# Causal mask of three chunks by ScalarE copies and GpSimd selects in place of VectorE products

## The chip, the cores and the metric

The kernel runs on one core of one Trainium2 chip. The metric is the device time of one execution in microseconds (us). Work is spread over TensorE (PE in the profile; its weight loads are PEld), VectorE (DVE), ScalarE (ACT), GpSimd (POOL) and the DMA queue of SyncE (SP). Each engine works its own queue in order and waits for others through semaphores.

## What is computed

A gated linear attention over 4 batches, 8 heads, 768 tokens and a head size of 48, followed by a two-layer block with hardswish on the 3072 tokens:

```python
for t in range(S):
    state = alpha[:, :, t, :, None] * state + einsum('bhd,bhe->bhde', k[:, :, t], v[:, :, t])
    y[:, :, t] = einsum('bhd,bhde->bhe', q[:, :, t], state)
x = y.transpose(0, 2, 1, 3).reshape(B * S, H * D)     # (3072, 384)
h = x @ w_in                                          # (3072, 2048)
g = h * clip(h + 3.0, 0.0, 6.0) / 6.0
out = g @ w_out                                       # (3072, 384)
```

## The kernel before

The 3072 tokens are cut into 24 chunks of 128 (`C`). A chunk `j` is six to a batch, and a chunk has two halves of 64 tokens (`HB`), `b` = 0 and 1. The 8 heads go as 4 pairs, `p` the pair and `a` the head in it. The recurrence is done by chunks: running products of `alpha` (scans on VectorE) scale `k` and `q`; inside a half, scores are a matmul of scaled `k` and `q`; what comes from earlier tokens goes through the state. The causal mask keeps a score only where the key's token is not later than the query's, so each 64x64 block of scores is multiplied by an upper triangle of ones.

Two chunks make a group `g` for the two matmul layers. Groups 0 and 1 run them plainly: `f` (L493) and `fa`, `fb` (L504) are pieces of the first layer, `fr` (L509, ScalarE) and `fg` (L513, VectorE) the hardswish, `b` (L531) pieces of the second. From group 2 on the first layer, and from group 1 on the second, use a scheme with fewer matmuls (`M`, L617; `P`, L720) and more sums on VectorE (`xc`, `y`, `o`, `s`, `x`). The weights come in as 64-bit floats and are turned to 32 bits on the chip in 16 slices (`w` loads; `d1`, `d2`, `dx` on ScalarE; `d3` on VectorE; `d4`, L216, on GpSimd) in the first 95 us.

All instructions follow one order written out by hand: a long string of words such as `m.3`, run under a manual schedule. Each word calls one step, and each engine gets its instructions in that order. The words that matter here:

- `sc.j.x.y`: scores of chunk j (L360) into PSUM banks x (heads a = 0) and y (a = 1) of four banks `t0` to `t3`
- `m.j`: the mask, `masked(j)` (L370), from these banks into the SBUF tile `A` (two buffers, `As`)
- `qa.j.b` (L380): copies of scaled `q` into the other partitions of `A`, on ScalarE
- `sv.j.b` (L433): copies of the state into the tile of `v`, on ScalarE
- `ya.j.x`, `yb.j` (L470): the matmuls of `A` and `v` for halves 0 and 1, into bank x; `cy` (L479) takes the result out
- `ta`, `tk`, `tq` (L283): transposes of alpha, k, q of the first six chunks into one of the same four banks; `ca` (L312) takes alpha out
- `u`, `sm`, `st`: update of the state (L444 on TensorE, L454 on VectorE, L423 on GpSimd)

`A` takes four mask products a chunk: one for each half b and head a, 64 partitions by 256 columns. Around the three changed steps the order reads (pieces left out at the dots):

```
... sv.3.0 qa.3.0 sm.3.0 w.9 f.0.6.3 qa.2.1 lk.5 d4.7 sv.3.1 tq.4.0 fb.0 m.3 sm.3.1 fr.0.1.0 ta.5.1 p.4
fg.0.1 d3.8 w.4 fr.0.5.1 ca.5 fg.0.5 fr.0.0.0 d1.8 ya.2.2 yb.2 w.10 d4.8 cy.2 fg.0.0 lq.5 ya.3.3 yb.3 cy.3
d2.9 la.6 f.0.7.2 ...
... sc.5.1.0 sc.4.3.2 u.4.3.0 u.5.1 d4.12 fa.4.3 d3.11 d4.11 m.4 fr.1.4.1 fr.1.2.0 f.1.5.0 fb.4 w.15 lq.6
sm.4.0 fg.1.2 b.0.0.1 ...
... d4.15 qa.5.1 m.5 kb.6.3 b.0.2 d4.14 P.1.0.0 sm.5.0 ...
```

Chunks 0 to 2 come before these, chunks 6 to 23 after them; the last product of the mask starts at 464.3 us.

Of the kernel before, what the change touches and what calls it, by code (L numbers as in the profile page):

```python
# [13 lines left out]
ALU = mybir.AluOpType  # L14
# [3 lines left out]
def kernel(  # L18
# [32 lines left out]
    nc = tc.nc  # L51
    B, H, S, D = q.shape
# [4 lines left out]
    NP = H // 2  # L57
# [5 lines left out]
    HB = C // 2  # L63
# [12 lines left out]
    mask = consts.tile([C, C], mybir.dt.bfloat16, tag="mask")  # L76
    make_upper_triangular(nc, mask, 1.0, diag=True)

    half = consts.tile([C, 1], FP, tag="half")
# [140 lines left out]
    R_t, P_t, Q_t, K_t, kb_t, A_t, xT_t, ps_t = ({} for _ in range(8))  # L220
# [131 lines left out]
    def scores(j, *at):  # L352
        sc = ps_t["sc", j] = [banks[i][:, 0 : NP * HB].rearrange("s (p t) -> s p t", p=NP)
                              for i in at]
        for p in range(NP):
            for b in range(2):
                half = slice(HB * b, HB * b + HB)
                for a in range(2):
                    r = slice(64 * a, 64 * a + D)
                    nc.tensor.matmul(sc[a][half, p], K_t[j][r, p, half], Q_t[j][r, p, half],  # L360
                                     start=True, stop=True)

    def masked(j):
        A_t[j] = As[j % 2]
        sc = ps_t.pop(("sc", j))
        for b in range(2):
            half = slice(HB * b, HB * b + HB)
            to = A_t[j][half, b].rearrange("s (p a) t -> s a p t", a=2)
            for a in range(2):
                nc.vector.tensor_tensor(  # L370
                    out=to[:, a], in0=sc[a][half],
                    in1=mask[half, half].unsqueeze(1).to_broadcast([HB, NP, HB]), op=ALU.mult)

    def place_q(j, b):
        if (j % NC, b) == (0, 0):
# [264 lines left out]
    def hidden1(g, o):  # L640
# [16 lines left out]
    b = {(i, k): w2[:, i * HF : (i + 1) * HF, k * HD : (k + 1) * HD]  # L657
         for i in range(2) for k in range(2)}
# [83 lines left out]
    def store2(g, i):  # L742
# [11 lines left out]
        "tq": lambda j, *i: transposed("q", j, *i), "ca": place_alpha, "r": decay, "p": growth,  # L754
        "k": lambda j: scaled("k", j), "q": lambda j: scaled("q", j),
        "sc": scores, "m": masked, "qa": place_q, "kb": k_by_token, "ck": keep_k,
        "st": decayed_state, "sv": place_state, "kt": turn_k, "kw": write_k, "kr": read_k,
        "u": update, "sm": next_state, "ya": lambda j, i: attend(j, 0, i),
# [196 lines left out]
```

## Time and profile before

| What | Value |
|---|---|
| Median of 3 runs | 530.98 us (530.96 to 531.14) |
| Profiled execution | 530.91 us, of which the span is 529.1 us |
| Instructions | 15082 |
| Granted TensorE clock (mean) | 0.999 |
| PE, PEld busy | 520.6 us (98%), 494.8 us (94%) |
| DVE, ACT, POOL busy | 462.0 us (87%), 259.6 us (49%), 55.3 us (10%) |
| Mask products, all chunks (L370) | 96, together 36.1 us |
| Mean rate of DMA | 103 GB/s |

The span runs from the first to the last instruction of the profiled execution; the time of the execution is somewhat longer. Busy time is the time in which an engine has an instruction in hand. Matmuls are pipelined and their ends modelled, so a full PE row has to be read together with the time that equal groups of matmuls take. In a timeline each line gives the start, the length, the engine, the line of the kernel, the operation with its tiles, and how often; a bracket at the end says how long the engine was idle before it and what ended that.

### The profile page before, as it was taken

To read this page: it belongs to the slowest core of one execution; us is meant where nothing else is said; L and a number is where in the kernel's file an instruction comes from. 1 tells how busy PE (TensorE), PEld (TensorE's weight loads), DVE (VectorE), ACT (ScalarE), POOL (GpSimd) and SP (SyncE) were. 2 spreads that over 40 slices of the span, in tenths; PEclk is the share of its full clock that TensorE was granted. 3 is DMA by queue.
4 is the path that set the end of the run, shared out by engine and by line. 5 is a ranking of instruction groups with operands and counts; after the bars stand their busy time and mean duration, and the time that the engine had idled before them with its cause. 6 is when DMAs were issued, how large, how long until landed. Compare 5 with 4: busy or idle time off the path is not lost.

```text
span 529.1 us, 15082 instructions
## 1 busy us (share of the span) xinstructions
PE 520.6 (98%) x6290; PEld 494.8 (94%) x6290; DVE 462.0 (87%) x838; ACT 259.6 (49%) x513; POOL 55.3 (10%) x89
## 2 busy tenths in 40 slices
PE   8799999999999999999999999999999999999997
PEld 6598886789999999999999999999999999999997
DVE  6998999999999999999999999899988896395471
ACT  4968875112755453464365355454353552543330
POOL 5333543100000100101000000000000000000000
PEclk9999999999999999999999999999999999999999
DMA  9998794213245365445452546153330214000001
GB/s 180 253 240 261 181 269 117 54 32 93 58 118 118 92 135 135 104 95 150 82 145 63 110 118 160 41 124 79 108 84 25 61 22 100 17 26 7 9 9 37
DMA packets 124100, 54.40 MB, mean 103 GB/s; under 512 B 83328, under 2 KB 116864, under 8 KB 124032
## 3 DMA queue, kind: packets, MB, share of 16 engines
q1 hardware_dynamic: 124032, 53.44, 42.8%
q8 instruction: 49, 0.80, 0.7%
q14 instruction: 19, 0.16, 0.1%
HBM read 44.50 MB, written 8.91 MB: 101 GB/s over the span
## 4 chain that ended last, share of the span: by engine, by line
PE 90%; DVE 4%; SPq 2%; DMA 2%; ACT 1%; issue 1%; POOL 0%; DVEq 0%; POOLq 0%; ACTq 0%
PE m_ps L720 36%; PE m_ps L617 31%; PE m_ps L493 6%; PE m_ps L531 4%; PE t_ps L470 4%; PE t_ps L360 2%; PE m_ps L504 2%; PE m_ps L548 2%; PE t_ps L444 1%; PE t_ps L283 1%; DMA rings<-in_alpha_dram 1%; DVE g_sb L554 1%; SPq L253 1%; PE t_ps L388 1%; SPq L410 0%
## 5 line engine op out<-in xcount | busy, mean ns | idle before, releaser
L720 PE MATMUL m_ps<-w,g_sb 128*128 128x192 f32 x704 | 121.8, 327 | 0.0
L623 ACT COPY g_sb<-m_ps 128x512 f32<-128x512 f32 x110 | 63.5, 583 | 116.6 <-PE m_ps L617 91.6
L720 PEld LDWEIGHTS m_ps<-w,g_sb 128*128 128x128 f32 x704 | 113.8, 190 | 0.5
L720 PE MATMUL m_ps<-rings,g_sb 128*128 128x192 f32 x528 | 91.3, 326 | 0.0
L720 PEld LDWEIGHTS m_ps<-rings,g_sb 128*128 128x128 f32 x528 | 85.4, 190 | 0.3
L617 PE MATMUL m_ps<-xc,w 128*128 128x128 f32 x640 | 82.1, 276 | 0.3 <-ACT g_sb L623 0.3
L617 PEld LDWEIGHTS m_ps<-xc,w 128*128 128x128 f32 x640 | 77.7, 192 | 1.2 <-ACT g_sb L623 0.4
L509 ACT ACTIVATE r<-g_sb,half 128x512 f32<-128x512 f32 x80 | 56.8, 721 | 36.3 <-DVE g_sb L558 17.5
L513 DVE SCALAR_TENSOR_TENSOR g_sb<-r,g_sb 128x512 f32<-128x512 f32 x80 | 53.8, 684 | 9.1 <-ACT r L509 8.7
L617 PE MATMUL m_ps<-xT,raw 128*128 128x128 f32 x400 | 53.2, 278 | 0.0
L617 PEld LDWEIGHTS m_ps<-xT,raw 128*128 128x128 f32 x400 | 48.8, 192 | 0.7 <-ACT g_sb L623 0.2
L664 DVE TENSOR_TENSOR g_sb<-g_sb 128x512 f32<-128x512 f32 (+1 forms) x55 | 42.2, 796 | 4.8 <-PE m_ps L720 4.5
L617 PE MATMUL m_ps<-xT,w 128*128 128x128 f32 x320 | 41.8, 277 | 0.0
L617 PEld LDWEIGHTS m_ps<-xT,w 128*128 128x128 f32 x320 | 39.0, 192 | 0.4
L380 ACT COPY A<-q 48x256 f32<-48x256 f32 x88 | 35.4, 402 | 2.9 <-PE t_ps L470 0.8
L370 DVE TENSOR_TENSOR A<-t_ps,mask 64x256 f32<-64x256 f32 x96 | 36.1, 415 | 0.4
L493 PE MATMUL m_ps<-xT,w 128*128 128x256 f32 x144 | 32.5, 381 | 0.0
L617 PE MATMUL m_ps<-xc,raw 128*128 128x128 f32 x240 | 31.9, 276 | 0.0
L321 DVE TENSOR_TENSOR_SCAN R<-t,ones 128x516 f32<-128x516 f32 x24 | 29.5, 1228 | 2.7 <-ACT t L312 2.7
L423 POOL TENSOR_TENSOR st<-sm,R 128x192 f32<-128x192 f32 x20 | 14.7, 737 | 157.2 <-DVE sm L454 157.1
L554 DVE TENSOR_TENSOR g_sb<-g_sb 128x512 f32<-128x512 f32 x40 | 26.9, 679 | 4.1 <-ACT g_sb L623 4.1
L554 DVE TENSOR_TENSOR g_sb<-m_ps,g_sb 128x512 f32<-128x512 f32 x30 | 20.5, 683 | 11.4 <-PE m_ps L617 7.0
(107 smaller groups left out, 718.2 us busy)
## 6 DMA issues: line engine op xcount, KB each, us to landing
raw<-in_moe_w_out_dram SPq DMA_DIRECT2D x8, 768.0 KB, 5.6
raw<-in_moe_w_in_dram SPq DMA_DIRECT2D x6, 768.0 KB, 6.8
v<-in_v_dram SPq DMA_DIRECT2D x48, 96.0 KB, 3.2
out_dram<-oh SPq DMA_DIRECT2D x44, 96.0 KB, 1.7
far<-kq SPq DMA_DIRECT2D x64, 64.0 KB, 2.2
kb<-far SPq DMA_DIRECT2D x64, 64.0 KB, 2.0
aq<-in_alpha_dram SPq DMA_DIRECT2D x36, 96.0 KB, 2.5
kq<-in_k_dram SPq DMA_DIRECT2D x36, 96.0 KB, 2.7
```

The costliest lines, as they stand in the source:

```text
L321: nc.vector.tensor_tensor_scan(out=reverse(R, n - 1, n), data0=reverse(ax, n, n), data1=reverse(ones, n, n), initial=0.0, op0=ALU.mult, op ...
L370: nc.vector.tensor_tensor(out=to[:, a], in0=sc[a][half], in1=mask[half, half].unsqueeze(1).to_broadcast([HB, NP, HB]), op=ALU.mult)
L380: nc.scalar.copy(out=to[:, a], in_=Q_t[j][64 * a : 64 * a + D, :, half])
L470: nc.tensor.matmul(y_of(j, (i + 1) // 2, p)[:, HB * b : HB * b + HB], vb[:, p, e : e + 32], A_t[j][:, b, 2 * p + a], start=(b == 0 and i = ...
L493: nc.tensor.matmul(h[:, f], w1[:, kk, o : o + C], xT_t[g][:, kk], start=(kk == 0), stop=(kk == KT - 1))
L509: nc.scalar.activation(out=to, in_=h, func=AF.Relu, bias=half, scale=1.0 / 6.0)
L513: nc.vector.scalar_tensor_tensor(out=to, in0=r, scalar=1.0, in1=h, op0=ALU.min, op1=ALU.mult)
L554: eng.tensor_tensor(out=out, in0=in0, in1=in1, op=ALU.add if s1 > 0 else ALU.subtract)
L617: nc.tensor.matmul(acc[g][i][:, f * C : (f + 1) * C], spots[w][:, f * C : (f + 1) * C], x_of(g, x), start=(first and f == 0), stop=last, s ...
L623: nc.scalar.copy(out=slots[z], in_=acc[g][i])
L664: nc.vector.tensor_tensor(out=out, in0=in0, in1=in1, op=ALU.subtract)
L720: nc.tensor.matmul(to[g], a, rhs[:, f], start=(first and f == 0), stop=(last and f == HF - 1), skip_group_check=True)
```

## The change

For chunks 3, 4 and 5, `masked` no longer multiplies scores by the mask on VectorE. ScalarE copies the unmasked scores from PSUM into `A` (four copies a chunk, same pieces of 64x256), and GpSimd then overwrites the entries of later keys with zero, in place, by two selects a chunk (one for each half, 64 partitions by 512 columns). GpSimd works only in SBUF here; so a chunk's 4 VectorE instructions become 4 of ScalarE and 2 of GpSimd. The order of words is the same, and the other 21 chunks are masked as before.

```diff
+    BY_SELECT = {3, 4, 5}
+
     def masked(j):
         A_t[j] = As[j % 2]
         sc = ps_t.pop(("sc", j))
...
             for a in range(2):
-                nc.vector.tensor_tensor(
-                    out=to[:, a], in0=sc[a][half],
-                    in1=mask[half, half].unsqueeze(1).to_broadcast([HB, NP, HB]), op=ALU.mult)
+                if j in BY_SELECT:
+                    nc.scalar.copy(out=to[:, a], in_=sc[a][half])
+                else:
+                    nc.vector.tensor_tensor(
+                        out=to[:, a], in0=sc[a][half],
+                        in1=mask[half, half].unsqueeze(1).to_broadcast([HB, NP, HB]), op=ALU.mult)
+        if j in BY_SELECT:
+            for b in range(2):
+                half = slice(HB * b, HB * b + HB)
+                nc.gpsimd.affine_select(out=A_t[j][half, b], in_=A_t[j][half, b],
+                                        pattern=[[0, H], [1, HB]], compare_op=ALU.is_ge, fill=0.0,
+                                        base=0, channel_multiplier=-1)
```

Lines behind the change lie 11 further down in the changed file (L380 becomes L391, and so on).

## The prediction

> **What bounds the kernel now.** First the page: busy times, their course over the span, and the chain that ended last.
>
> ```profile
> PE 520.6 (98%) x6290; PEld 494.8 (94%) x6290; DVE 462.0 (87%) x838; ACT 259.6 (49%) x513; POOL 55.3 (10%) x89
> ...
> PE   8799999999999999999999999999999999999997
> PEld 6598886789999999999999999999999999999997
> DVE  6998999999999999999999999899988896395471
> ...
> PE 90%; DVE 4%; SPq 2%; DMA 2%; ACT 1%; issue 1%; POOL 0%; DVEq 0%; POOLq 0%; ACTq 0%
> ```
>
> TensorE carries the chain; VectorE is as full as TensorE in the first half. Since matmul ends are modelled, a full PE row does not prove that PE is at its pace; the steps do. In the chain in order of time, 48 matmuls of L493 take 10.36 us (216 ns each), as 12 of them take 2.59 us elsewhere (216), and the groups of 16 at L720 take 2.60 us each nearly everywhere. So PE runs at its own pace, and time that it loses after the first 30 us comes back only from its few later stalls. The list of waits names those:
>
> ```profile
> PE t_ps L470 <- DVE s L454: 0.4, 1, 0.4
> PE m_ps L617 <- ACT g_sb L623: 0.3, 1, 0.3
> ```
>
> Columns: total us, times, longest. They lie at 183.25 us (0.36) and 275.90 us (0.25); together 0.6 us is all that a freer VectorE could win back. Then the timeline around m.3, the first changed step (start, us, engine):
>
> ```profile
> 46.82 0.58 ACT L392 COPY kb<-t_ps 128x512 f32<-128x512 f32 x1 [1.84 <-PE t_ps L388]
> ...
> 47.85 1.52 DVE L370 TENSOR_TENSOR A<-t_ps,mask 64x256 f32<-64x256 f32 x4
> ...
> 49.10 1.66 ACT L380 COPY A<-q 48x256 f32<-48x256 f32 x4
> ...
> 49.30 1.50 PE L504 MATMUL m_ps<-xT,w 128*128 128x128 f32 x12
> ...
> 50.64 0.60 PE L283 MATMUL t_ps<-ident,rings 128*128 128x128 f32 x4
> 50.78 0.73 ACT L433 COPY v<-s 48x192 f32<-48x192 f32 x2
> ...
> 51.17 1.99 PE L470 MATMUL t_ps<-A,v 128*32 128x64 f32 x128
> 51.53 1.26 ACT L509 ACTIVATE r<-m_ps,half 128x512 f32<-128x512 f32 x2
> ...
> 52.26 0.69 DVE L513 SCALAR_TENSOR_TENSOR g_sb<-r,m_ps 128x512 f32<-128x512 f32 x1 [1.36 <-ACT r L509]
> ```
>
> The reader should see that VectorE finished m.3 at 49.37, that ScalarE worked without a gap from 46.82 through 51.5, and that PE began ta.5.1 (L283) at 50.64 with no wait.
>
> **Step m.3: the one that costs.** Scores of chunk 3 lie in banks 2 and 1 (sc.3.2.1). ta.5.1 writes its four transposes into bank 1, and ya.2.2 behind it writes bank 2. Before, both banks were read out at 49.37, 1.27 us ahead of need. In the changed program the first transpose of ta.5.1 carries one more wait, on ScalarE: the last of the four copies reads bank 1.
>
> The queue decides when that is. m.3 stands behind qa.3.0, qa.2.1 and sv.3.1 in the order, so the copies follow the second L433 copy, which ends at 51.51. One copy is 64x256 from PSUM; no such row exists. Neighbours by size, ScalarE copies from PSUM: 128x192 takes 318 ns (L737), 128x384 480 (L479), 128x512 583 (L623), so 256 comes to about 370. Three L623 copies in a row take 1.56 us, one each 0.49, 0.09 less than their length: copies from PSUM overlap. L380 (48x256, SBUF) takes 402 ns and steps by 0.42. So the step is 0.28 to 0.42; I take 0.28, since the source is PSUM: 51.45 + 3 x 0.28 + 0.37 = 52.66; with the upper value 51.53 + 3 x 0.42 + 0.40 = 53.19. PE restarts 0.05 to 0.2 us after such a releaser (VectorE's k at 18.87 let L388 go at 18.92; its s at 183.10 let L470 go at 183.25). That gives 52.7 to 53.4 in place of 50.64: a stall of 2.1 to 2.75 us. I take 2.25, near the PSUM rows.
>
> What else is late at that point, and is it later than PE?
> - The gate fr.0.1.0 (L509) waits behind the four copies: from 51.53 to about 52.75. Its product fg.0.1 (L513) releases bank m2 for f.0.7.2 (L493 at 53.09); before, product end (52.95) and matmul start were 0.14 apart. The release comes at 52.75 + 1.42 = 54.2. PE gets there at 52.9 + 0.44 (ta) + 1.92 (L470, as in the chain) = 55.25. Covered by 1 us; without that cover it alone costs 1.2 us, the lower bound of this step.
> - The two selects. The first starts after copy 2, at 52.1; ya.3 needs it, yb.3 needs the second. Nearest rows: the setup's affine select of 128x128 takes 292 ns, a memset of 128 columns 204, of 1024 columns 951. With the memset's fixed part of 97 ns, the select costs 1.52 ns a column, so 512 cost 0.88 us; a memset of 64x512 takes 0.52 (lower end), and two-input L216 of 768 columns takes 1.46 to 2.65, or 1.0 to 1.77 for 512 (upper end). I take 0.9, by the select's own row. The second then ends at 53.95, and PE reaches yb.3 at 52.9 + 0.44 + 0.96 + 0.48 = 54.8. Covered by 0.8 us; it comes through from 1.3 us a select on.
> - ScalarE and VectorE themselves are set back by about 1.2 us (VectorE's freed 1.5 us only lengthens its wait of 1.36 us on L509), less than PE. GpSimd's next L216 (d4.8, 55.14) starts after the selects.
>
> **Steps m.4 and m.5: nothing either way.** The copies of m.4 wait for sc.4 (L360 at 75.36 plus 1.16, now 2.25 later) and stand ahead of fr.1.4.1 and fr.1.2.0, and sm.4.0 on VectorE now waits for them; the product fg.1.2 slips by 2.25 plus 0.2 to 0.6 to about 82.3. Its bank m1 is wanted by b.0.0.1, at 82.5 + 2.25: 2.4 us in hand. ScalarE has 2.82 us idle at 82.73 and takes up the rest; A of chunk 4 is not read until 111.5. GpSimd's d4.13 (83.91), queued behind these selects, starts after they end; SP's queue is unchanged. The copies of m.5 fall into ScalarE's idle 9.03 us before 98.67, the selects into GpSimd's 3.35 us before 93.82. VectorE is freed of 1.52 us at 93.61 and then waits on PE at 119.99, as it already did for 1.37 us:
>
> ```profile
> 119.99 0.36 DVE L740 TENSOR_TENSOR oh<-m_ps,p 128x192 f32<-128x192 f32 x1 [1.37 <-PE m_ps L720]
> ```
>
> There VectorE is back where it was against PE, so the stalls at 183 and 276 us stay. PE has no stall between 53 and 119 us that the freed 3 x 1.52 = 4.6 us of VectorE could take away; they are worth 0.
>
> **Sum.** The profiled execution took 530.91 us, of which 529.1 is the span and 1.8 lies around it; the median of the runs is 530.98, 0.07 more. 530.9 + 2.25 = 533.2 us.
>
> **Rivals.**
> - *Selects on the path.* At 1.77 us each the second ends at 52.1 + 3.54 = 55.65, yb.3 starts 0.85 late, total stall 3.1: 534.1; with the upper copy step 534.6. Against it: the setup's two selects start 0.24 us apart. For it: the same L216 takes anything from 1.46 to 2.65 us. Chance 0.12.
> - *Clock.* PE's first 4.8 us ran at half pace: four transposes took 0.85 us in the chain at 4.81, later 0.44. If a pause brings that back for as long, it costs some 2.4 us more: 535.6. Against it: between 17.9 and 21.26 us PE stood still for 1.02 and then 1.46 us, and the four transposes after that took 0.63 in the timeline against 0.60 in flow. Chance 0.04.
>   The Trainium skill, "TensorE: Matmul & The Clock Gate", Part 1, puts the return to half clock at an idle window of about 3.4 us; by that rule this gap is too short, and the trace agrees as far as its own pauses go.
> - *Faster.* VectorE is 98% busy from 60 to 100 us (19.71 and 19.68 of 20 us). Were it the true bound there, with PE's row full only by modelled ends, the 3.0 us freed by m.4 and m.5 would count and m.3 would cost only ScalarE's 1.2: 529.1. It decides if PE waits unseen for VectorE between 60 and 119 us; against it stand the equal steps of 216 ns and no such wait in the list. Chance 0.05.
>   The Trainium skill, "Perfetto Trace Analysis", Optimizing Scalar/DVE Operations, holds that a saturated VectorE may be relieved onto ScalarE or even GpSimd; here that helps only if this rival is right.
> - *No loss.* The stall is made good later, if PE's later order has slack that I do not see, or ScalarE reaches the copies earlier: 530.9 to 531.9. Against it: ScalarE had no gap from 46.82 on, PE next to none after 53. Chance 0.09.
>
> **How the numbers follow.** My forecast has 0.70, with its own range of 532.4 (the stalls at 183 and 276 vanish) to 533.7 (slow copies). Selects take the top to 534.8. Out of 531.8 to 534.8 fall the clock, the faster case and most of "no loss", with edges under 0.2. A change under 0.2% (1.06 us) cannot be told from none: faster 0.05, same 0.09, slower 0.86.
>
> **What would show it.** Right: a wait of PE at L283 on ScalarE's new copies, 2.1 to 2.75 us long and ending near 53, the only new one in the list; L493 at 55.3 in place of 53.09, and everything of PE after that shifted by the same amount; ScalarE copies stepping by about 0.28. Wrong: L470 waiting on GpSimd there (selects), L493 groups of 12 above 2.59 us after the gap (clock), fewer than 2 us lost by PE at 119, or PE ahead of its old times after 95 (VectorE was the bound).

## The result, and the profile after

The changed kernel takes 533.09 us (median of 5 runs, 532.74 to 533.89) against 530.98 us (530.58 to 531.45): 2.11 us more, a ratio of 1.0042 with a 95% interval of 1.0027 to 1.0057. The profiled execution took 533.60 us, its span is 531.9.

The page after, the lines that answer to those of before:

```profile
PE 521.8 (98%) x6290; PEld 495.5 (93%) x6290; DVE 460.8 (87%) x826; ACT 263.4 (50%) x525; POOL 60.6 (11%) x95
...
PE 87%; DVE 4%; DMA 3%; SPq 2%; ACT 2%; issue 1%; DVEq 0%; POOL 0%; ACTq 0%; POOLq 0%
```

PE has the same 6290 matmuls and almost the same busy time (521.8 against 520.6 us). VectorE lost 12 instructions, and its mask products fell from 36.1 to 31.6 us, yet its busy time fell by only 1.2 us; the last section says where most of the rest went. The waits of PE after (total us, times, longest):

```profile
PE t_ps L283 <- ACT A L373: 1.9, 1, 1.9
...
PE t_ps L481 <- DVE s L465: 0.4, 1, 0.4
PE m_ps L628 <- ACT g_sb L634: 0.2, 1, 0.2
```

The first line is new, and is the transposes of ta.5.1 waiting for chunk 3's copies. The other two are the stalls near 183 and 276 us, still there. The timeline of the changed kernel around m.3 (11 lines have been added, so L380 is L391, L470 is L481, L493 is L504):

```profile
49.67 1.65 ACT L391 COPY A<-q 48x256 f32<-48x256 f32 x4
...
49.87 1.50 PE L515 MATMUL m_ps<-xT,w 128*128 128x128 f32 x12
...
51.33 0.71 ACT L444 COPY v<-s 48x192 f32<-48x192 f32 x2
51.95 1.29 ACT L373 COPY A<-t_ps 64x256 f32<-64x256 f32 x4
52.65 1.38 POOL L381 TENSOR_SCALAR_AFFINE_SELECT A<-A 64x512 f32<-64x512 f32 x2 [2.80 <-ACT A L373]
53.27 1.27 ACT L520 ACTIVATE r<-m_ps,half 128x512 f32<-128x512 f32 x2
...
53.30 0.66 PE L283 MATMUL t_ps<-ident,rings 128*128 128x128 f32 x4 [1.92 <-ACT A L373]
...
53.88 1.99 PE L481 MATMUL t_ps<-A,v 128*32 128x64 f32 x128
53.99 0.69 DVE L524 SCALAR_TENSOR_TENSOR g_sb<-r,m_ps 128x512 f32<-128x512 f32 x1 [3.04 <-ACT r L520]
...
55.81 2.43 PE L504 MATMUL m_ps<-xT,w 128*128 128x256 f32 x10
```

The copies follow the last L444 copy at once and end at 53.24; PE starts 0.06 us later. The 12 matmuls of L515 ahead of this start at 49.87, which is 0.57 us later than before: that much of this one execution was lost earlier. So ta.5.1 is late by 53.30 - 50.64 - 0.57 = 2.09 us on account of the change. The list gives its wait as only 1.92 us, because a wait is counted from the end of the matmuls before it (51.37), and undisturbed ta.5.1 began 0.16 us ahead of that end (50.64 against 49.30 + 1.50). At the other end the loss is unchanged: VectorE's L740, which stood at 119.99, is at 122.67 here, 2.68 later, of which 2.11 after taking off the 0.57.

### The profile page after: what moved, and what is told of

Its sections match the earlier page's. It is cut to its first block, busy times and chain, and to the rows that moved or that the text cites. A ratio compares the mean times of both kernels' runs of the same rounds, so it can differ in the third digit from the quotient of the medians.

```text
span 531.9 us, 15095 instructions
## 1 busy us (share of the span) xinstructions
PE 521.8 (98%) x6290; PEld 495.5 (93%) x6290; DVE 460.8 (87%) x826; ACT 263.4 (50%) x525; POOL 60.6 (11%) x95
## 4 chain that ended last, share of the span: by engine, by line
PE 87%; DVE 4%; DMA 3%; SPq 2%; ACT 2%; issue 1%; DVEq 0%; POOL 0%; ACTq 0%; POOLq 0%
PE m_ps L731 36%; PE m_ps L628 31%; PE m_ps L504 5%; PE m_ps L542 4%; PE t_ps L481 4%; PE t_ps L360 2%; PE m_ps L515 2%; SPq L253 1%; PE t_ps L455 1%; DMA rings<-in_q_dram 1%; DMA rings<-in_alpha_dram 1%; DVE g_sb L565 1%; PE t_ps L283 1%; ACT A L391 1%; PE t_ps L399 1%
## 5 line engine op out<-in xcount | busy, mean ns | idle before, releaser
L628 PE MATMUL m_ps<-xT,raw 128*128 128x128 f32 x400 | 53.2, 278 | 0.0
L675 DVE TENSOR_TENSOR g_sb<-g_sb 128x512 f32<-128x512 f32 (+1 forms) x55 | 43.5, 819 | 4.8 <-PE m_ps L731 4.5
L391 ACT COPY A<-q 48x256 f32<-48x256 f32 x88 | 35.4, 402 | 2.6 <-PE t_ps L481 0.8
L504 PE MATMUL m_ps<-xT,w 128*128 128x256 f32 x144 | 32.5, 381 | 0.0
L375 DVE TENSOR_TENSOR A<-t_ps,mask 64x256 f32<-64x256 f32 x84 | 31.6, 414 | 0.3
```

What stands on the lines that cost most here:

```text
L375: nc.vector.tensor_tensor(out=to[:, a], in0=sc[a][half], in1=mask[half, half].unsqueeze(1).to_broadcast([HB, NP, HB]), op=ALU.mult)
L391: nc.scalar.copy(out=to[:, a], in_=Q_t[j][64 * a : 64 * a + D, :, half])
L504: nc.tensor.matmul(h[:, f], w1[:, kk, o : o + C], xT_t[g][:, kk], start=(kk == 0), stop=(kk == KT - 1))
L628: nc.tensor.matmul(acc[g][i][:, f * C : (f + 1) * C], spots[w][:, f * C : (f + 1) * C], x_of(g, x), start=(first and f == 0), stop=last, s ...
L675: nc.vector.tensor_tensor(out=out, in0=in0, in1=in1, op=ALU.subtract)
```

## The experiments

Two theories were to be told apart. *Queue*: the loss is PE's one wait at ta.5.1, because the copies stand late in ScalarE's order. *Selects*: GpSimd's part costs, by late tiles or by slowing VectorE beside it. All ratios are to the kernel before on the same chip.

**Which chunk.**

```diff
-    BY_SELECT = {3, 4, 5}
+    BY_SELECT = {4, 5}      # e1_only_4_5
+    BY_SELECT = {3}         # e2_only_3
```

> Chunk 3 is masked on VectorE again; 4 and 5 by copies and selects. Queue theory (the loss is PE's one wait of 1.9 to 2.1 us for chunk 3's copies, which stand late in ScalarE's order): no wait at the transposes of ta.5.1, time of before, 530.8 to 531.3. Rival theory (GpSimd's selects cost, by slowing VectorE's instructions beside them or by late tiles, in all three chunks alike): two thirds of the loss stay, 532.3 to 532.6. Rival that VectorE was the true bound at 60 to 100 us: faster, 528 to 530.

> Only chunk 3 by copies and selects. Queue theory: the whole loss is there, 532.9 to 533.4, with the same wait of PE at ta.5.1. Select theory: one third of the loss, 531.5 to 531.9.

Measured: e1_only_4_5 531.02 us, ratio 0.9998 (0.9986 to 1.0010); e2_only_3 533.32 us, ratio 1.0046 (1.0033 to 1.0060). Chunk 3 alone has the whole loss; chunks 4 and 5 cost and bring nothing that shows (the interval of e1_only_4_5 runs from 0.7 us less to 0.5 us more). PE waits 1.9 us for the copies in e2_only_3, and not at all in e1_only_4_5.

**The same copies elsewhere in ScalarE's order.** `mc.3` is the four copies, `ms.3` the two selects, which stay where `m.3` was.

```diff
-    ... d4.6 ck.4 sm.2.1 st.3 d2.8 ...            tq.4.0 fb.0 m.3 sm.3.1 ...
+    ... d4.6 ck.4 sm.2.1 st.3 mc.3 d2.8 ...       tq.4.0 fb.0 ms.3 sm.3.1 ...   # e3_copies_before_d2
+    ... d4.6 sm.2.1 mc.3 ck.4 st.3 d2.8 ...       tq.4.0 fb.0 ms.3 sm.3.1 ...   # e4_copies_before_ck
```

> All three chunks as in the changed kernel, but chunk 3's four copies stand earlier in ScalarE's order: ahead of d2.8, where ScalarE has no idle time after them; the selects stay where they were. Queue theory: banks 1 and 2 are read out at about 48.7, so ta.5.1 doesn't wait; but everything of ScalarE behind them comes 1.25 us later, the gate fr.0.1.0 too, and so f.0.7.2 waits for its bank m2: PE loses 1.2 in place of 2.1 us, 532.0 to 532.4. If the loss were the selects': as the changed kernel, 533.1. If a late gate costs nothing: 531.0.

> As the changed kernel, but chunk 3's four copies stand ahead of ck.4 (and sm.2.1 ahead of them), where ScalarE was idle for 1.84 us before the change; the selects stay where they were. Queue theory: four copies take 1.3 us, so nothing behind them is late and no bank is: time of before, 530.8 to 531.4, with all 12 VectorE products still gone. Select theory: as the changed kernel, 533.1. If VectorE were the bound anywhere behind: faster than before, under 530.

Measured: e3_copies_before_d2 532.24 us, ratio 1.0018 (1.0005 to 1.0030); e4_copies_before_ck 530.89 us (530.59 to 533.29), ratio 0.9999 (0.9985 to 1.0013). The loss of e3_copies_before_d2 is 1.0 us by the ratio (0.3 to 1.6) and 1.3 us by the medians. Its timeline (two lines further down again, so L493 is L506):

```profile
47.08 1.30 ACT L373 COPY A<-t_ps 64x256 f32<-64x256 f32 x4
...
50.41 0.60 PE L283 MATMUL t_ps<-ident,rings 128*128 128x128 f32 x4
...
52.51 1.26 ACT L522 ACTIVATE r<-m_ps,half 128x512 f32<-128x512 f32 x2
53.23 0.69 DVE L526 SCALAR_TENSOR_TENSOR g_sb<-r,m_ps 128x512 f32<-128x512 f32 x1 [3.04 <-ACT r L522]
...
53.97 0.70 PE L506 MATMUL m_ps<-xT,w 128*128 128x256 f32 x2 [0.86 <-DVE g_sb L526]
```

ta.5.1 no longer waits; now the late gate holds bank m2, and PE waits there. In e4_copies_before_ck the copies run in what was ScalarE's idle time ahead of `ck.4` (L392 before, L405 here), and nothing behind is late:

```profile
44.84 1.29 ACT L373 COPY A<-t_ps 64x256 f32<-64x256 f32 x4
...
46.43 0.58 ACT L405 COPY kb<-t_ps 128x512 f32<-128x512 f32 x1 [0.31 <-PE t_ps L401]
```

The same 12 copies and 6 selects then cost nothing. Nor do the 12 products taken from VectorE bring anything.

**The selects.** Left out altogether, and three times for chunk 3.

```diff
-        if j in BY_SELECT:                                   # before the selects
+        if False:                                            # e5_no_selects
...
+                for _ in range(3 if j == 3 else 1):          # e6_selects_3x
                     nc.gpsimd.affine_select(...)
```

> The changed kernel without any select: chunks 3 to 5 keep scores of later keys. Queue theory: time unchanged, 532.9 to 533.4, same wait at ta.5.1. Select theory: back to 531.0. In the trace, VectorE's two-input sums that ran beside selects (the L692 pair at 93.6, 1.74 us in the changed kernel) should take their 1.29 us again.

> Each select of chunk 3 is issued three times (the repeats change nothing). In the changed kernel the two selects end at 54.03 and yb.3 needs the second at 55.32, so 1.3 us of cover. Six selects at 0.70 us a step from 52.65 end at 56.85: yb.3 waits 1.5 us, 534.4 to 534.9, with PE waiting on GpSimd at L481. If selects overlap or are never waited for: 533.1.

Measured: e5_no_selects 533.23 us, ratio 1.0043 (1.0031 to 1.0055): the selects as they are cost nothing. e6_selects_3x 537.41 us, ratio 1.0126 (1.0109 to 1.0142): they do cost once they are long enough. PE then waits for them at yb.3:

```profile
57.57 0.65 PE L482 MATMUL t_ps<-A,v 128*32 128x64 f32 x32 [1.27 <-POOL A L382]
```

But the time is some 2.5 us above what was expected.

**The copies twice**, which lengthens the wait of ta.5.1; the gate and the selects move with it.

```diff
+                    for _ in range(2 if j == 3 else 1):
                         nc.scalar.copy(out=to[:, a], in_=sc[a][half])
```

> Each copy of chunk 3 is issued twice. Queue theory: the last one ends 4 steps of 0.31 us later, so PE waits 3.1 to 3.3 us at ta.5.1 in place of 1.9 to 2.1: 534.2 to 534.6. If something else released ta.5.1: 533.1.

Measured: 536.03 us (534.88 to 537.38), ratio 1.0097 (1.0082 to 1.0112). The wait grew to 3.5 us, a little more than expected: the eight copies took 2.89 us, 0.36 a step, where each piece is written twice in a row. That accounts for 0.2 to 0.4 of the excess over 534.2 to 534.6 us. In the profiled execution (537.21 us) the rest is in the clock. Two-microsecond stretches of e7_copies_2x (busy time of PE, PEld, DVE, ACT, POOL, then granted clock, DMA share, GB/s):

```profile
52.00:54.00 2.00, 0.00 (x0) 0.00 (x0) 0.00 (x0) 1.88 (x7) 0.66 (x1) 0.80 1.02 387
54.00:56.00 2.00, 1.81 (x36) 1.48 (x39) 1.12 (x2) 1.98 (x5) 0.66 (x1) 0.50 1.21 216
56.00:58.00 2.00, 2.00 (x84) 2.00 (x80) 1.93 (x4) 1.73 (x3) 0.14 (x1) 0.50 1.18 160
58.00:60.00 2.00, 2.00 (x38) 1.65 (x28) 0.82 (x2) 1.05 (x2) 1.62 (x3) 0.50 0.08 20
```

The granted clock fell to a half at 53.2 us, still in the pause, and was back at full at 60.0. The profiled executions of e5_no_selects and e6_selects_3x show one such spell after their pause of 1.9 us, here e5_no_selects:

```profile
54.00:56.00 2.00, 2.00 (x88) 2.00 (x82) 1.93 (x4) 2.00 (x4) 0.00 (x0) 0.50 1.17 258
56.00:58.00 2.00, 2.00 (x48) 1.75 (x41) 1.72 (x3) 1.36 (x4) 1.35 (x1) 0.67 1.31 167
```

and its 128 matmuls of L481 took 3.47 in place of 1.99 us. That execution took 534.95 us and another 534.75; the other four of the six were at 532.67 to 533.38. In e2_only_3, 8 of 12 executions lie at 532.77 to 533.53 and 4 at 534.16 to 534.77; the five of the changed kernel all lie at 532.74 to 533.89. So 6 of 23 executions with the pause of 1.9 us are in an upper group. Only one of the six was profiled, so that the other five had the same spell is inferred. Without this pause such stragglers are rarer: 2 of all 74 executions of the kernel before (532.35 and 534.56), 1 of 12 of e4_copies_before_ck (533.29).

**VectorE freed for nothing.** Chunks 4 and 5 without any mask, all else as before; this leaves out part of the computation.

```diff
-    BY_SELECT = {3, 4, 5}
+    BY_SELECT = set()
...
-            for a in range(2):
+            for a in range(0 if j in (4, 5) else 2):
```

> The kernel before, but chunks 4 and 5 have no mask products at all (their part of A keeps old values), which frees VectorE of 3.0 us around 77 and 94 us and gives no engine anything in exchange. Queue theory (TensorE is the bound there): within 0.3 us of before, 530.7 to 531.3. Rival that VectorE is the bound between 60 and 100 us: up to 3 us faster, 528 to 529.

Measured: 530.91 us, ratio 0.9998 (0.9989 to 1.0006). The mask products fell by 3.0 us where VectorE is 98% busy. About half of that came back, because two sums now ran beside GpSimd (last section): VectorE's busy time fell from 462.0 to 460.4 us. Still 1.6 us were freed, and the time does not move; the interval leaves at most 0.6 us.

**The pause filled.** Matmuls on the identity into bank t3, whose result nobody reads, ahead of ta.5.1 (n = 4, 7, 4 and 2).

```diff
+    def fill(n):
+        for _ in range(n):
+            nc.tensor.matmul(banks[3].rearrange("p (a c) -> p a c", c=C), ident,
+                             ident.unsqueeze(1).to_broadcast([C, 4, C]), start=True, stop=True)
...
-    ... fr.0.1.0 ta.5.1 ...
+    ... fr.0.1.0 zt.n ta.5.1 ...
```

> The changed kernel, with four matmuls of 128x512 on the identity into the unused bank t3 ahead of ta.5.1: they keep TensorE busy for 1.7 us of its wait for the copies, and their result is never read. Clock theory (some executions lose a further 1.7 us because the pause halves the clock for about 3.4 us; executions of e2_only_3 and e5_no_selects fall into two groups, 532.7 to 533.5 and 534.2 to 534.95): time at the lower group, 532.7 to 533.4, and no granted clock under 1.00 between 50 and 62 us. If the upper group has another cause (DMA, VectorE): two groups again.

> Chunk 3's copies twice, as in e7_copies_2x, with seven such filling matmuls (3.0 us) ahead of ta.5.1. Clock theory: the wait of 3.5 us stays and the half clock after it goes: 534.3 to 534.7, against 536.0 without filling. Otherwise: 536.0 as before.

> Chunk 3's selects three times, as in e6_selects_3x (537.4), with four filling matmuls ahead of ta.5.1. Clock theory: without half clock the two waits of 1.9 and 1.3 us and the restarts after them remain, and since PE then gets to yb.3 earlier its wait for GpSimd grows to 2.3 us at most: 534.3 to 535.6, no execution above 536. Otherwise: 537.4.

Measured: e9_fill 534.54 us (534.29 to 535.37), ratio 1.0068 (1.0055 to 1.0082); e10_copies_2x_fill 536.96 us (536.82 to 537.10), ratio 1.0111 (1.0098 to 1.0125); e11_selects_3x_fill 535.90 us (535.43 to 536.10), ratio 1.0090 (1.0076 to 1.0104). The filling was mis-sized: each product became two instructions of 0.43 us, so four took 3.4 us and seven 6.0, and both ran past the copies. The timeline of e9_fill:

```profile
51.15 3.60 PE L564 MATMUL t_ps<-ident 128*128 128x512 f32 x8
...
54.59 0.60 PE L283 MATMUL t_ps<-ident,rings 128*128 128x128 f32 x4
```

So e10_copies_2x_fill does not answer its question, but it gives the price of lateness alone: counted from the 12 matmuls ahead of it, ta.5.1 starts 6.0 us late (56.81), and the time is 6.0 us longer, at a mean granted clock of 1.0 (0.999 once). And e9_fill tells what was asked, against e7_copies_2x. Behind matmuls ta.5.1 starts 3.4 us late, and this costs 3.6 us (3.3 to 4.4) at a mean granted clock of 1.0 in each of the 5 executions. Behind a pause it starts 3.7 us late, and this costs 5.1 us (3.9 to 6.4) at 0.994 to 0.997. In e11_selects_3x_fill, too, the median falls by 1.5 us against e6_selects_3x, though PE there reaches yb.3 no earlier and waits 1.2 us for the same selects. It lies above the 534.3 to 535.6 that were expected, and two of its four executions are above 536.

> As e9_fill, but half the filling: a 128x512 product on the identity turned out to be two instructions of 0.43 us each, so two of them fill 1.7 us (four took 3.4 and ran past the copies). ta.5.1 then waits about 0.4 us more for the copies. Clock theory: 532.7 to 533.5 in every execution, none at 534.2 or above, granted clock 1.00 from 50 to 62 us. If the upper group has another cause, some executions are above 534 again.

Measured: 533.22 us (532.69 to 533.73), ratio 1.0041 (1.0027 to 1.0055); PE waits 0.2 us for the copies behind the filling. No execution of the five is above 534 (533.73, the longest, is a little above the 533.5 expected), and the granted clock is 1.00 from 50 to 62 us in the profiled one. Filled or not, the changed kernel's normal loss is the 2.1 us of late copies; what the filling seems to take away is the chance of a spell of half clock behind it. Five executions without one are weak evidence by themselves, where 6 of 23 are in the upper group.

## Why the prediction was right, point by point

- *Bound.* "PE runs at its own pace" held: e8_no_mask_4_5 and e1_only_4_5 are both at 0.9998, and their intervals leave at most 0.7 us of gain. The rival that VectorE was the true bound, with a time of 529.1 us, is refuted.
- *The place.* The new wait of ta.5.1 on the last copy of m.3, with the copies behind qa.2.1 and sv.3.1, is what the profile shows, and chunk 3 alone carries the loss.
- *The size.* With the 0.57 us of the start taken off, the copies run from 51.38 to 52.67 (forecast 51.45 to 52.66), step 0.31 (0.28), length 367 ns (370). PE restarts 2.09 us late; 2.25 had been taken, 0.16 too much. From an end at 52.66 the 2.25 us mean a restart after 0.23 us, outside the prediction's own 0.05 to 0.2; PE followed after 0.06. The sign that was named, a wait of 2.1 to 2.75 us in the list, came out as 1.92, for the reason told with the result. L493, forecast for 55.3, is at 55.81 - 0.57 = 55.24. That it fits so well is partly luck: the restart was set 0.16 us too late, and ta.5.1 was given 0.44 us where it took 0.58 (53.30 to 53.88).
- *Cover.* The gate was covered: its product ends at 54.68 - 0.57 = 54.11 (forecast 54.2), 1.1 us ahead of L493. Without that cover it costs by itself: 1.2 us forecast, 1.0 by the ratio and 1.3 by the medians in e3_copies_before_d2. The selects take 0.69 us each in place of 0.9 and were covered with more to spare.
- *m.4 and m.5.* Nothing, as forecast, but one term was wrong. VectorE was to be freed of 1.52 us at 93.61 and to spend it waiting on PE at L740, where it had waited 1.37 us. The wait fell instead:

```profile
122.67 0.36 DVE L751 TENSOR_TENSOR oh<-m_ps,p 128x192 f32<-128x192 f32 x1 [0.17 <-PE m_ps L731]
```

  It is 1.55 us in e2_only_3, where 4 and 5 are masked on VectorE, and 1.12 in e5_no_selects. So VectorE came out 1.4 us later against TensorE for being relieved of m.4 and m.5. Half of it is m.4, where the product fg.1.2 waits for the gate behind ScalarE's copies: it starts at 82.23 in place of 81.52 in e2_only_3. The other half is m.5, where 2.2 us came back for 1.5 saved (last section). The time is unharmed because 0.17 us of the wait were left.
- *Clock.* This was the weak point: given 0.04, with the pauses of 1.02 and 1.46 us at 18 to 21 us as evidence against it. The changed kernel's own profile takes that evidence away, for it shows the half clock behind two such pauses (1.02 and 1.22 us, the second up to 21.43):

```profile
22.00:24.00 2.00, 2.00 (x35) 1.58 (x35) 2.00 (x2) 1.97 (x2) 1.97 (x3) 0.50 0.82 152
24.00:26.00 2.00, 2.00 (x10) 1.41 (x9) 1.54 (x5) 1.26 (x2) 1.51 (x1) 0.65 1.00 330
```

  The four transposes behind the second pause took 0.63 us in this execution too, as in the one before: the half clock began only behind them, at 22.0, so their time could not tell. What tells is the four matmuls of 128x384 (L548, L559 after) that follow: 2.50 us in place of 1.34. The granted clock has to be read together with such times: it says 1.00 for the first 4.8 us as well, where the pace was half. Here the spell costs little, since TensorE waits for others in that stretch anyway. Behind ta.5.1 nothing hides it, and the upper groups of e2_only_3 and e5_no_selects lie 1.3 and 1.9 us above the lower ones. That is also less than the 2.4 us of the prediction's rival. The case is one of chance from execution to execution, not of either-or: the five of the changed kernel stayed in the lower group, the median was safe, the top of the range less so.

Why the spell comes in some executions and not in others, and why four of the five executions of e6_selects_3x lie at 537.38 to 539.35 where one pause of 1.9 and one of 1.3 us with one spell gave 535.91, stays open; their mean granted clocks (0.99 to 0.997) point the same way, but only one execution has a timeline. One reading fits the profiled executions and is not shown. The spells last 3.4 us, or twice that. In e5_no_selects and e6_selects_3x the whole pause of 1.9 us lies in the 3.4 us ahead of the spell. In the changed kernel and e2_only_3, whose profiled executions had a spell at 22.0 and 21.8 us and none behind ta.5.1, steps of 3.41 us from there put an edge at about 52.7 and 52.5 us, in the middle of the pause, with no more than 1.4 us of it on one side. So it may matter where a pause falls against such steps.

## What to carry to other kernels

Moving work off a busy engine has a price on the engine that takes it, and the price is read from that engine's queue at that place: here four copies of 0.3 us each cost 2.1 us behind ready work, 1.0 to 1.3 us in front of a gate, and nothing in an idle stretch two words earlier. Ask first which buffer the moved instruction releases, and who wants that buffer next. TensorE had no wait on VectorE between 53 and 119 us, and there relief was worth nothing, although VectorE was 98% busy. Nor is the time of the instructions that were taken away the time that is freed: what moves up in their place may run slower there.

## What the runs showed of the hardware that was not expected

- **Half clock after short pauses.** A single pause of 1.9 us of TensorE, with some work on either side, was enough for a spell of half clock of about 3.4 us (e5_no_selects: mean 0.98 from 52 to 54 us, 0.50 from 54 to 56, 0.67 from 56 to 58). Behind the pause of 3.5 us of e7_copies_2x it lasted 6.8 us, twice as long. The Trainium skill, "TensorE: Matmul & The Clock Gate", Part 1, speaks of an idle window of about 3.4 us, and says that this window runs freely. The length fits such a window, and so does a spell that comes in some executions only; but the pauses that triggered it were shorter than 3.4 us, and the measurement decides.
- **VectorE and GpSimd slow each other.** The freed time of m.5 went there. Before, GpSimd's L216 at 93.82 ran beside the mask products, which read PSUM and were not slowed (1.52 us for four). With those gone, two sums of two SBUF operands fall beside it. The same pair before and after:

```profile
93.61 1.52 DVE L370 TENSOR_TENSOR A<-t_ps,mask 64x256 f32<-64x256 f32 x4
93.82 1.46 POOL L216 TENSOR_TENSOR w<-raw 128x768 int32<-128x768 int32 x1 [3.35 <-issue]
...
95.43 1.28 DVE L664 TENSOR_TENSOR g_sb<-g_sb 128x512 f32<-128x512 f32 x2
```

```profile
97.98 1.47 POOL L216 TENSOR_TENSOR w<-raw 128x768 int32<-128x768 int32 x1 [2.14 <-issue]
98.03 2.57 DVE L675 TENSOR_TENSOR g_sb<-g_sb 128x512 f32<-128x512 f32 x2
```

  L216 itself kept its 1.47 us. The selects of m.5, beside two other such sums, took 2.17 us for the pair in place of 1.38, and stretched those sums from 1.29 to 1.74; in e5_no_selects these take 1.29 again. So the 1.5 us saved on VectorE came back as 1.3 us beside L216 and 0.9 beside the selects (0.45 on those sums, 0.46 on the L206 that follows them: 0.55 before, 1.01 after). At m.3 it was the same with the scan L333, which came to run beside an L216 and took 2.05 in place of 1.22 us.
